# First pair's q and k ahead of V, a VectorE mask for two pairs, and earlier casts in a windowed-attention and tanh-MLP kernel

## The chip, the cores and the metric

The kernel runs on one core of one Trainium2 chip. The metric is the device time of one execution in microseconds. Before the change it is 363.07 us, the median of three runs (362.23 to 364.77). The execution that was profiled took 361.24 us, and its trace spans 359.5 us from the first to the last instruction, at a mean granted TensorE clock of 0.967 of full speed.

Engines are named as in the profile: PE is the matrix engine (PEld its weight loads), DVE is VectorE, ACT is ScalarE, POOL is GpSimd, SP is SyncE. SP and ACT start DMAs through hardware descriptor generation (HWDGE), POOL through software descriptor generation (SWDGE).

## What is computed

Eight sequences (batches) of 576 positions, eight heads of 64. Attention is causal with a window of 64: a query sees itself and the 63 keys before it. The heads' outputs are put side by side (4608 tokens of 512), multiplied by w_in, passed through h - tanh(h), and multiplied by w_out. All inputs and the output are float32.

```python
def _attn_ref(q, k, v):                       # [8, 8, 576, 64] each
    scores = np.matmul(q, k.transpose(0, 1, 3, 2)) / np.sqrt(64)
    rel = pos[:, None] - pos[None, :]
    scores = np.where((rel >= 0) & (rel < 64), scores, -1e9)
    attn = softmax(scores)
    return np.matmul(attn, v)

def _moe_ref(x, w_in, w_out):                 # x: [4608, 512]
    h = x @ w_in                              # [4608, 2048]
    return (h - np.tanh(h)) @ w_out
```

## The kernel before

**Attention.** Work goes by head pair: pair g is batch g // 4, heads p and p + 4 of it, so there are 32 pairs. q and k of a pair are loaded with 96 rows of 6 positions (`load`, line 86), transposed on PE, and copied out of PSUM to `kT` and `qs` or `qT`. Queries are cut into nine blocks j of 64; block j needs the 128 keys that end with it. Scores come out transposed (keys on the partitions), ACT takes the exponential into `PT`, and a second matmul multiplies by v with a column of ones added, so the sum of the weights arrives with the product and DVE divides by it (`reciprocal` and `tensor_tensor`). Results go to `xs`, are transposed (`x_tr`) and land in `xT` for the MLP.

**Two forms.** The first two batches use head-by-head transposes of the loaded tile (`tr_heads`, line 240), and `tile_scores` (267), which hides the forbidden keys before the exponential: two extra matmuls of the tile `hide` with the identity add -2^30 to them in PSUM (line 271). Values come from `tile_pv` (283). From batch 2 on q and k are first cast to a layout with both heads side by side (`cast`, 107), transposed (`tr`, 250), scored without hiding (`scores`, 298), and multiplied by a 0/1 mask on DVE afterwards (`masking`, 306). That mask is a 128x64 bf16 tile which lives in PSUM bank 5 and is written once by a PE transpose of `seen` (`see`, 208). The last batch's transposes are made by DMA.

**v.** It is loaded with 72 rows of 8 positions, cast to `vb` (`cast_v`, 160), and copied by small DMAs inside SBUF into windows `vw`: `keys_v` (164) fills the lower half of each block's 128 keys, and `shift_v` on DVE (169) copies block j to the upper half of block j + 1; later batches get both halves by `windows_v` (153). For batch 0 v is loaded as float32 on the SP and ACT queues (`load_v_wide`, 145), while q and k come over POOL's queue and are cast to bf16 by the DMA.

**The MLP.** Tokens go in nine chunks of 512. For each of 16 slices of 128 hidden features, four matmuls with w_in make `h` (line 361), ACT takes tanh (366), DVE subtracts (`gT`, 373). Output rows are made by four times 16 matmuls with w_out (385), copied by ACT and stored.

**What sets the order.** The schedule is by hand (`tc.manual_schedule()`): every engine runs its instructions in the order in which the program issues them, and waits only for data and buffers. The program has two parts. A prologue (422 to 476) does the attention of batch 0: loads, 13 matmuls on zeros that keep PE busy (`warm`, 235), casts, transposes, scores, values. Then a loop runs over numbered slots (607): `OPS` says which group of four MLP matmuls stands in a slot (slots 0 to 31 hold w_in of chunk 0, 32 to 47 w_out of chunk 0, 48 to 63 w_in of chunk 1, 64 to 79 w_out of chunk 1, from 80 on w_in of chunk 2 and then w_in and w_out alternating), and `at(h, ...)` puts a piece of attention behind it. `std` (530) places a pair of batch 2 or 3: casts at `ck` and `cq`, transposes at `t` and `tk`, scores at `ss`, masking at `ms`, values at `p`. Casts of q and k for pairs 8 and 9 are on DVE, later ones on POOL. `pace` (411) makes POOL wait for a given slice of `gT` before it issues a batch's loads. There is one buffer for v (`vall`), one `vb`, three each for the cast tiles, and one PSUM bank (3) for most transposes.

Of the kernel before, what the change touches and what calls it, by code (L numbers as in the profile page):

```python
# [7 lines left out]
F32 = mybir.dt.float32  # L8
BF16 = mybir.dt.bfloat16
ALU = mybir.AluOpType  # L10
# [5 lines left out]
def kernel(  # L16
# [9 lines left out]
    nc = tc.nc  # L26
# [14 lines left out]
    ctx.enter_context(tc.manual_schedule())  # L41

    const = ctx.enter_context(tc.tile_pool(name="const", bufs=1))
    all_pool = ctx.enter_context(tc.tile_pool(name="all", bufs=2))
    v_pool = ctx.enter_context(tc.tile_pool(name="v", bufs=1))
    row_pool = ctx.enter_context(tc.tile_pool(name="row", bufs=3))
# [9 lines left out]

    ident = const.tile([128, 128], BF16, name="ident")
    tick = const.tile([1, 1], BF16, name="tick")
    seen = const.tile([64, 128], BF16, name="seen")
    mask = ps[:, 5, 480:512].bitcast(BF16)  # L60
    hide = const.tile([128, 2, 64], BF16, name="hide")
    WIDE = 1024, 1024
    w_in_sb = [const.tile([128, 4, n], BF16, name=f"wi{i}") for i, n in enumerate(WIDE)]
# [16 lines left out]
    def move(eng, o, i):  # L80
        if eng is nc.scalar:
            nc.scalar.activation(o, i, ACT.Copy)  # L82
        else:
            eng.tensor_copy(o, i)  # L84

    def load(g, n, eng):

        b, pr = divmod(g, NP)
        if (b, n) not in whole:
            whole[b, n] = all_pool.tile([P, H, E * D], BF16, tag=n, name=n + "all")  # L90
        t = whole[b, n][:, pr::NP]
        eng.dma_start(out=t, in_=(q if n == "q" else k)[b, pr::NP].rearrange("h (p e) d -> p h (e d)", e=E))  # L92
        stage[g, n] = t

# [47 lines left out]
        for pr in range(NP):  # L142
            stage[b, pr, "v"] = t[:, pr::NP]

    def load_v_wide(pr, eng):
        if (0, "v") not in whole:
            whole[0, "v"] = g_pool.tile([128, M, TOK], BF16, tag="gT", name="v32").rearrange("p m t -> p (m t)").bitcast(F32)[
                0:PV].rearrange("p (h c) -> p h c", h=H)
        t = whole[0, "v"][:, pr::NP]
        eng.dma_start(out=t, in_=v[0, pr::NP].rearrange("h (p e) d -> p h (e d)", e=EV))  # L150
        stage[0, pr, "v"] = t

    def windows_v(b, j, eng):
        if j == 0:
            keys_v(b, 0, eng)
        else:
            eng.dma_start(out=vw[b % 2][:, j].rearrange("p h c -> p (h c)"),
                          in_=vb[8 * j - 8:8 * j + 8].rearrange("p e h c -> p e (h c)"))

    def cast_v(b, pr, eng=nc.gpsimd):  # L160
        move(eng, vb[:, :, 2 * pr:2 * pr + 2, 0:D].rearrange("p e h d -> p h e d"),
             stage.pop((b, pr, "v")).rearrange("p h (e d) -> p h e d", d=D))
# [43 lines left out]
                                base=64, pattern=[[-1, 128]], channel_multiplier=1)  # L206

    def see():
        nc.tensor.transpose(mask, seen, ident[0:64, 0:64])

    nc.vector.memset(qT[0], 0.0)
    nc.vector.memset(ident, 0.0)
# [22 lines left out]
    def warm(n):  # L235

        for _ in range(n):
            nc.tensor.matmul(ps[:, 7, :], qT[0][:, 0, 0:128], qT[0][:, 0, 0:512], start=True, stop=True)
# [25 lines left out]
        a, b = banks  # L264
        return ps[:, a:b + 1:b - a]

    def tile_scores(g, grp, banks):

        j0, n = (0, 5) if grp == 0 else (5, 4)
        for h in range(2):  # L270
            nc.tensor.matmul(ps[:, banks[h], 0:64 * n], ident, hide[:, h].unsqueeze(1).to_broadcast([128, n, 64]),  # L271
                             start=True, stop=False)
        for i in range(n):
            j = j0 + i
            for h in range(2):
                r = slice(64 * h, 64 * h + 64)
                nc.tensor.matmul(ps[:, banks[h], 64 * i:64 * i + 64], kT[g % NR][r, 64 * j:64 * j + 128],  # L277
                                 qs[g % 2][r, 64 * j:64 * j + 64], start=False, stop=i == n - 1)
        o = PT[g % NPT][:, j0:j0 + n].rearrange("p j (h t) -> p h j t", h=2)
        nc.scalar.activation(o, pair_of(banks)[:, :, 0:64 * n].rearrange("p h (j t) -> p h j t", t=64),  # L280
                             ACT.Exp, scale=scale)

    def tile_pv(g, banks):

# [67 lines left out]
    gT = {}  # L352
# [55 lines left out]
    def at(h, fn, *args):  # L408
        items.setdefault(h, []).append((fn, args))
# [9 lines left out]

    V, A, G, Y = nc.vector, nc.scalar, nc.gpsimd, nc.sync  # L420

    for pr in range(NP):
        load_v_wide(pr, (Y, A)[pr % 2])
    load(0, "k", G)
    load(0, "q", G)
    make_ident()
    load(1, "k", G)
    load(1, "q", G)
# [2 lines left out]
    load(2, "k", G)  # L431
    load(2, "q", G)

    warm(13)
    for pr in range(NP - 1):
        cast_v(0, pr, V)
    cast_v(0, 3, A)
    for j, eng in enumerate((Y, G, A, G, Y, A, G, Y, G)):
        keys_v(0, j, eng)
    for n in "kq":  # L440
        load(3, n, G)
# [7 lines left out]
        load(g, "q", G)  # L449
    load(7, "k", G)  # L450

    tr_heads(0, "k", 2, V)
    tr_heads(0, "q", 3, A)
    tile_scores(0, 0, (0, 1))
    tile_scores(0, 1, (4, 5))
    tr_heads(1, "k", 2, V)
    tr_heads(1, "q", 3, A)
    tr_heads(2, "k", 2, V)
    tile_scores(1, 0, (0, 1))
    tile_scores(1, 1, (4, 5))  # L460
    tr_heads(2, "q", 3, V)
    shift_dve(0, 0, 4)
    tile_pv(0, (6, 7))
    tr_heads(3, "k", 2, V)
    tile_scores(2, 0, (0, 1))
    tile_scores(2, 1, (4, 5))
    tr_heads(3, "q", 3, A)
    tile_pv(1, (6, 7))
    tile_scores(3, 0, (0, 1))
    tile_scores(3, 1, (4, 5))  # L470
    x_tr(0, 0, 0, 4, 0, A)
    x_tr(0, 0, 4, 9, 1, A)
    tile_pv(2, (2, 3))
    tile_pv(3, (6, 7))
    x_tr(0, 1, 0, 4, 4, V)
    x_tr(0, 1, 4, 9, 5, A)

    at(32, more_constants)
    at(33, lambda: [cast_v(1, pr, V) for pr in range(NP)])
    at(34, see)  # L480
    at(35, lambda: [keys_v(1, j, G) for j in range(NJ)])
    at(35, load, 7, "q", G)
    at(35, load_v_all, 2)
# [31 lines left out]
    for g in 10, 11:  # L515
        at(49, load, g, "k", G)
        at(49, load, g, "q", G)
    at(60, load_v_all, 3)
    for g in range(12, 16):
        at(g + 49, load, g, "k", G)  # L520
        at(g + 49, load, g, "q", G)
    for i in range(2):
        at(76 + 2 * i, more_zeros, i)

    def whole_pv(g):
        for i in range(3):
# [1 line left out]
        norm(g)  # L528

    def std(g, ck, cq, t, tk, ss, ms, p):  # L530
        at(ck, cast, g, "k", V if g < 10 else G)
        at(cq, cast, g, "q", V if g < 10 else G)
        at(t, tr, g, "q", 3, A, V)
        at(tk, tr, g, "k", 3, A)
        for i in range(3):
            at(ss + 2 * i, scores, g, i, 4)
        at(ms, masking, g)
        at(p, whole_pv, g)

    for i, g in enumerate(range(8, 12)):  # L540
        a = (50, 55, 60, 65)[i]
        std(g, a - 1, a - 2 if i < 2 else a - 2, a, a + 2, a + 3, a + 8, a + (12 if i == 0 else 11))
    at(70, x_tr, 2, 0, 0, 4, 3, V)
    at(71, x_tr, 2, 0, 4, 9, 3, A)
    at(78, x_tr, 2, 1, 0, 4, 3, V)
# [2 lines left out]
    for g in range(3 * NP, B * NP):  # L548
        b, pr = divmod(g, NP)
        a = 8 * g - 48 - (0, 2, 4)[min(b - 3, 2)]  # L550
        s = 32 * b - (0, 2, 4)[min(b - 3, 2)]
        cv, ky = s - 72 + 5 * pr, s - 54
        if b == 3:
            a = (65, 71, 76, 81)[pr]
            cv = 63 + pr
        elif b == 4:
            a = 82 + 7 * pr
            cv, ky = 74 + 3 * pr, 85
        elif b == 5:
# [97 lines left out]
```

The softmax here doesn't subtract the row's maximum and nothing guards it: scores larger than these inputs give would overflow.

## Time and profile before

| engine | busy us | share of the span |
|---|---|---|
| PE | 322.7 | 90% |
| DVE | 196.3 | 55% |
| ACT | 184.8 | 51% |
| POOL | 113.5 | 32% |

PE's busy time is mostly the MLP's: 145.1 us for w_in (576 matmuls) and 139.6 us for w_out. A busy time is the union of the intervals in which instructions of a kind run, so it counts a matmul at half clock twice as long. The page cuts the span into 40 slices of 9 us; the digits are tenths of the slice:

```profile
PE   5777999789776979699999999998999999999995
...
POOL 6730154757851742280172325801000000000000
PEclk9559999999999889999999999999999999999999
DMA  7999969696879146905769599488830410010021
```

Slices 1 and 2 (9 to 27 us) are at a clock of 0.5, two slices in the middle at 0.8. The DMA engines are busy for nine tenths from 9 us on until 45 us.

The groups of the operations that the change moves, adds or drops:

| operation | count in the stretch | mean ns |
|---|---|---|
| DVE cast of v to `vb`, 72x1024 from float32 | 3 | 700 |
| ACT cast of v to `vb`, 72x1024 from float32 | 1 | 1088 |
| PE `hide` matmul, 128x320 and 128x256, first 46 us | 8 and 8 | 444 and 375 |
| DVE mask multiply, 128x1152, whole run | 24 | 746 |
| POOL cast of q or k, 96x768 | 40 | 829 and 834 |
| DVE cast of q or k, 96x768 | 4 | 346 |

### The profile page before, as it was taken

The numbers are of one execution on the slowest core, as the hardware profiler recorded it, in microseconds if no ns is written. First come the engines' busy times: TensorE is split into PE (matmuls) and PEld (weight loads), VectorE is DVE, ScalarE is ACT, GpSimd is POOL, SyncE is SP. The second block draws the span as 40 slices with busy tenths as digits, with TensorE's granted clock in tenths as the row PEclk, the third lists the DMA queues.
The fourth block names the chain that finished last, engine by engine and source line by source line (L and its number), as shares of the span: only waits on it lengthen the run. The fifth ranks groups of instructions, "written<-read, shape, count | busy, mean of one in ns | idle before, by whom it ended". The sixth has DMA issues, their size and how long they took to land.

```text
span 359.5 us, 6211 instructions
## 1 busy us (share of the span) xinstructions
PE 322.7 (90%) x2407; PEld 178.0 (50%) x2438; DVE 196.3 (55%) x317; ACT 184.8 (51%) x334; POOL 113.5 (32%) x168
## 2 busy tenths in 40 slices
PE   5777999789776979699999999998999999999995
PEld 1454545546443445465555555554555444444442
DVE  3255743667834477867677666655666334433300
ACT  1445715478543558556666666654554443444411
POOL 6730154757851742280172325801000000000000
PEclk9559999999999889999999999999999999999999
DMA  7999969696879146905769599488830410010021
GB/s 175 155 199 216 195 107 155 103 180 99 128 115 255 44 81 102 170 3 113 137 120 184 112 151 191 100 145 191 203 109 30 96 60 29 29 60 29 29 79 70
DMA packets 51310, 42.69 MB, mean 119 GB/s; under 512 B 20848, under 2 KB 44080, under 8 KB 51280
## 3 DMA queue, kind: packets, MB, share of 16 engines
q0 software_dynamic: 21072, 19.77, 35.9%
q1 hardware_dynamic: 29752, 21.79, 24.9%
q10 hardware_dynamic: 456, 0.72, 0.7%
q8 instruction: 19, 0.31, 0.3%
q14 instruction: 11, 0.09, 0.1%
HBM read 36.70 MB, written 11.21 MB: 133 GB/s over the span
## 4 chain that ended last, share of the span: by engine, by line
PE 74%; DVE 8%; DMA 7%; ACT 5%; issue 2%; POOL 2%; ACTq 1%; SPq 0%; DVEq 0%; POOLq 0%
PE ps L385 33%; PE ps L361 28%; DMA qall<-in_q_dram 4%; PE ps L314 3%; PE ps L302 3%; DMA v<-in_v_dram 2%; PE ps L254 2%; DVE xs L325 2%; DVE gT L373 2%; PE ps L246 2%; PE ps L271 1%; ACT th L366 1%; PE ps L277 1%; DVE xs L296 1%; PE ps L331 1%
## 5 line engine op out<-in xcount | busy, mean ns | idle before, releaser
L361 PE MATMUL ps<-xT,wi 128*128 128x512 bf16 x576 | 145.1, 381 | 3.8 <-DVE gT L373 3.1
L373 DVE TENSOR_TENSOR gT<-ps,th 128x512 bf16<-128x512 f32 x144 | 98.4, 691 | 85.6 <-ACT th L366 83.8
L385 PE MATMUL ps<-w_out_sb,gT 128*128 128x512 bf16 x545 | 139.6, 382 | 2.4 <-issue 0.8
L366 ACT ACTIVATE th<-ps 128x512 f32<-128x512 f32 x144 | 85.7, 598 | 75.1 <-PE ps L361 73.3
L361 PEld LDWEIGHTS <-wi 128*128 128x128 bf16 x576 | 61.7, 113 | 51.1 <-issue 5.6
L385 PEld LDWEIGHTS <-gT 128*128 128x128 bf16 x576 | 53.7, 98 | 56.2 <-issue 2.0
L304 ACT ACTIVATE pt<-ps 128x384 bf16<-128x384 f32 x72 | 35.3, 490 | 38.0 <-PE ps L302 37.8
L84 POOL COPY vb<-vall 72x1024 bf16<-72x1024 bf16 x24 | 25.0, 1055 | 42.5 <-DMA vall<-in_v_dram 30.9
L325 DVE TENSOR_TENSOR xs<-ps,rc 64x576 bf16<-64x576 f32 x48 | 36.2, 755 | 1.1
L390 ACT ACTIVATE ysb<-ps 128x512 f32<-128x512 f32 x36 | 21.6, 599 | 21.9 <-PE ps L385 21.7
L302 PE MATMUL ps<-qt,kt 128*128 128x128 bf16 x216 | 24.0, 220 | 3.5 <-ACT pt L304 1.6
L314 PEld LDWEIGHTS <-pt 128*128 128x128 bf16 x216 | 16.7, 98 | 15.3 <-issue 2.0
L314 PE MATMUL ps<-vw,pt 128*128 128x130 bf16 x216 | 21.4, 220 | 2.3 <-DVE xs L325 1.9
L302 PEld LDWEIGHTS <-kt 128*128 128x128 bf16 x216 | 16.5, 98 | 13.0 <-issue 3.6
L84 DVE COPY qt<-ps 64x576 bf16<-64x576 bf16 x20 | 15.2, 760 | 13.5 <-ACT qt L82 13.4
L84 POOL COPY qb<-qall 96x768 bf16<-96x768 bf16 x18 | 14.9, 829 | 14.6 <-DMA qall<-in_q_dram 14.6
L308 DVE TENSOR_TENSOR pt<-pt,ps 128x1152 bf16<-128x1152 bf16 x24 | 17.9, 746 | 1.4 <-ACT pt L304 1.4
L84 POOL COPY kb<-kall 96x768 bf16<-96x768 bf16 x22 | 18.2, 834 | 0.0
L280 ACT ACTIVATE pt<-ps 128x640 bf16<-128x640 f32 (+1 forms) x16 | 10.3, 650 | 13.9 <-PE ps L277 13.9
L84 DVE COPY kt<-ps 128x576 bf16<-128x576 bf16 x8 | 6.0, 756 | 18.4 <-PE ps L246 18.4
L92 POOL DMA_DIRECT2D kall<-in_k_dram x16 | 11.2, 702 | 11.0 <-DMA wi<-in_moe_w_in_dram 5.4
L82 ACT ACTIVATE kt<-ps 128x576 bf16<-128x576 bf16 x20 | 13.0, 648 | 2.0 <-PE ps L254 1.9
(64 smaller groups left out, 195.8 us busy)
## 6 DMA issues: line engine op xcount, KB each, us to landing
out_dram<-ysb SPq DMA_DIRECT2D x36, 256.0 KB
vw<-vb SPq DMA_DIRECT2D x40, 130.0 KB
vall<-in_v_dram POOLq DMA_DIRECT2D x7, 576.0 KB, 10.0
kall<-in_k_dram POOLq DMA_DIRECT2D x16, 144.0 KB, 7.4
qall<-in_q_dram POOLq DMA_DIRECT2D x16, 144.0 KB, 7.4
kall<-in_k_dram POOLq DMA_DIRECT2D x4, 576.0 KB, 6.3
qall<-in_q_dram POOLq DMA_DIRECT2D x4, 576.0 KB, 8.6
wi<-in_moe_w_in_dram POOLq DMA_DIRECT2D x2, 1024.0 KB, 13.5
```

Source lines behind the costliest of these rows:

```text
L82: nc.scalar.activation(o, i, ACT.Copy)
L84: eng.tensor_copy(o, i)
L302: nc.tensor.matmul(sp[:, i, :], kT[g % NR][:, 64 * j:64 * j + 128], qT[g % NR][:, :, 64 * j:64 * j + 64], start=True, stop=True)
L304: nc.scalar.activation(PT[g % NPT][:, 3 * grp:3 * grp + 3, :], sp, ACT.Exp, scale=scale)
L308: nc.vector.tensor_tensor(p, p, mask.unsqueeze(1).to_broadcast([128, 2 * NJ, 64]), ALU.mult)
L314: nc.tensor.matmul(ps[:, 5 + grp, 130 * i:130 * i + 130], PT[g % NPT][:, j, :], vw[b % 2][:, j, 2 * pr:2 * pr + 2, :], start=True, stop=True)
L325: nc.vector.tensor_tensor(xo[r, :, :, pr, :], ov[r, :, :, h, 0:D], rc[r].to_broadcast([64, 3, 3, 64]), ALU.mult)
L361: nc.tensor.matmul(hp, w_in_tile(ki, m), chunk_tile(c)[:, :, ki % 2, 64 * (ki // 2):64 * (ki // 2) + 64], start=(ki == 0), stop=(ki == 3))
L366: nc.scalar.activation(th, hp, ACT.Tanh)
L373: nc.vector.tensor_tensor(gT[c][:, m, :], hp, th, ALU.subtract)
L385: nc.tensor.matmul(yp, gT[c][:, m, s * 128:(s + 1) * 128], w_out_sb[:, m, :], start=(m == 0), stop=(m == M - 1))
L390: nc.scalar.activation(ysb, ps[:, yp_bank(c, s), :], ACT.Copy)
```

## The change

It has four parts.

1. **Start.** The first pair's q and k are loaded first, as float32, q on SP's and k on ACT's queue, and cast by DVE and ACT (`cast_flat`). The four loads of v move to POOL's queue, which casts to bf16 (`load_v`), ahead of the other pairs. `warm` shrinks from 13 to 9 matmuls. The casts of v to `vb` all go to DVE, behind the first pair's k copy and ahead of the others. The small DMAs of v's keys are issued after the first pair's scores, five on POOL, three on SP and one on ACT (before: four, three and two).
2. **Mask.** `tile_scores` has three forms. Pair 0 hides as before. Pairs 1 and 2 ("mask") leave out the hiding matmuls, and DVE multiplies `PT` by the mask after the exponential. For pair 3 ("hidden") the hiding matmuls stand ahead of the scores as a step of their own. So `see` runs in the prologue, with a 128x128 `seen`, and the mask moves within bank 5. Pair 0's values come after pair 2's scores, pairs 1 to 3 follow together, and two `warm` matmuls stand between the two halves of the final transposes.
3. **Casts.** In batches 2 and 3 the casts come three to six slots ahead of the transposes (before: one and two), q ahead of k. Those of pairs 12, 13 and 14 go from POOL to DVE; 10, 11 and 15 stay on POOL.
4. **Slots.** Loads of v and of pairs 12 to 15 are issued earlier, the transposes of batch 3 start at slots 68, 73, 78 and 82 (before 65, 71, 76 and 81), batch 4's two slots later, and the memsets of `qz` move from slots 76 and 78 to 140 and 144.

The diff, cut to what these parts need:

```diff
+    qk_pool = ctx.enter_context(tc.tile_pool(name="qk", bufs=1))
...
-    seen = const.tile([64, 128], BF16, name="seen")
-    mask = ps[:, 5, 480:512].bitcast(BF16)
+    seen = const.tile([128, 128], BF16, name="seen")
+    mask = ps[:, 5, 448:480].bitcast(BF16)
...
-        if (b, n) not in whole:
-            whole[b, n] = all_pool.tile([P, H, E * D], BF16, tag=n, name=n + "all")
-        t = whole[b, n][:, pr::NP]
+        if g == 0:
+            t = qk_pool.tile([P, 2, E * D], F32, tag=n, name=n + "f")
+        else:
+            if (b, n) not in whole:
+                whole[b, n] = all_pool.tile([P, H, E * D], BF16, tag=n, name=n + "all")
+            t = whole[b, n][:, pr::NP]
...
-    def load_v_wide(pr, eng):
-        if (0, "v") not in whole:
-            whole[0, "v"] = g_pool.tile([128, M, TOK], BF16, tag="gT", name="v32").rearrange("p m t -> p (m t)").bitcast(F32)[
-                0:PV].rearrange("p (h c) -> p h c", h=H)
-        t = whole[0, "v"][:, pr::NP]
-        eng.dma_start(out=t, in_=v[0, pr::NP].rearrange("h (p e) d -> p h (e d)", e=EV))
-        stage[0, pr, "v"] = t
+    def load_v(b, pr):
+        if (b, "v") not in whole:
+            whole[b, "v"] = v_pool.tile([PV, H, EV * D], BF16, tag="v", name="vall")
+        t = whole[b, "v"][:, pr::NP]
+        nc.gpsimd.dma_start(out=t, in_=v[b, pr::NP].rearrange("h (p e) d -> p h (e d)", e=EV))
+        stage[b, pr, "v"] = t
...
+    def cast_flat(g, n, eng):
+        t = row_pool.tile([P, E, 2, D], BF16, tag=n + "b", name=n + "b").rearrange("p e h d -> p (e h d)")
+        t = t.rearrange("p (h c) -> p h c", h=2)
+        move(eng, t, stage.pop((g, n)))
+        stage[g, n] = t
...
-    def tile_scores(g, grp, banks):
+    def tile_scores(g, grp, banks, how="hide"):
...
+        if how == "hide":
+            hides(grp, banks)
...
+        if how == "mask":
+            p = PT[g % NPT][:, j0:j0 + n].rearrange("p j (h t) -> p (j h) t", h=2)
+            nc.vector.tensor_tensor(p, p, mask.unsqueeze(1).to_broadcast([128, 2 * n, 64]), ALU.mult)
...
+    load(0, "q", Y)
+    load(0, "k", A)
     for pr in range(NP):
-        load_v_wide(pr, (Y, A)[pr % 2])
-    load(0, "k", G)
-    load(0, "q", G)
+        load_v(0, pr)
     make_ident()
...
-    warm(13)
-    for pr in range(NP - 1):
+    warm(9)
+    cast_flat(0, "q", V)
+    cast_flat(0, "k", A)
+    tr_heads(0, "k", 2, V)
+    tr_heads(0, "q", 3, A)
+    see()
+    for pr in range(NP):
         cast_v(0, pr, V)
-    cast_v(0, 3, A)
-    for j, eng in enumerate((Y, G, A, G, Y, A, G, Y, G)):
+    tile_scores(0, 0, (0, 1))
+    tile_scores(0, 1, (4, 5))
+    for j, eng in enumerate((Y, G, A, G, Y, G, G, Y, G)):
         keys_v(0, j, eng)
...
-    tile_scores(1, 0, (0, 1))
-    tile_scores(1, 1, (4, 5))
-    tr_heads(2, "q", 3, V)
+    tile_scores(1, 0, (0, 1), "mask")
+    tile_scores(1, 1, (4, 5), "mask")
+    tr_heads(2, "q", 3, A)
+    tile_scores(2, 0, (0, 1), "mask")
+    tile_scores(2, 1, (4, 5), "mask")
+    tr_heads(3, "k", 2, V)
     shift_dve(0, 0, 4)
     tile_pv(0, (6, 7))
-    tr_heads(3, "k", 2, V)
-    tile_scores(2, 0, (0, 1))
-    tile_scores(2, 1, (4, 5))
     tr_heads(3, "q", 3, A)
+    hides(0, (0, 1))
+    hides(1, (4, 5))
+    tile_scores(3, 0, (0, 1), "hidden")
+    tile_scores(3, 1, (4, 5), "hidden")
     tile_pv(1, (6, 7))
...
+    warm(2)
...
-    at(60, load_v_all, 3)
+    at(49, load_v_all, 3)
     for g in range(12, 16):
-        at(g + 49, load, g, "k", G)
-        at(g + 49, load, g, "q", G)
+        at(60 + (g - 12) // 2, load, g, "k", G)
+        at(60 + (g - 12) // 2, load, g, "q", G)
     for i in range(2):
-        at(76 + 2 * i, more_zeros, i)
+        at(140 + 4 * i, more_zeros, i)
...
-        at(ck, cast, g, "k", V if g < 10 else G)
-        at(cq, cast, g, "q", V if g < 10 else G)
+        at(cq, cast, g, "q", V if g not in (10, 11, 15) else G)
+        at(ck, cast, g, "k", V if g not in (10, 11, 15) else G)
...
         if b == 3:
-            a = (65, 71, 76, 81)[pr]
-            cv = 63 + pr
+            a = (68, 73, 78, 82)[pr]
+            cv = 62 + pr
         elif b == 4:
-            a = 82 + 7 * pr
-            cv, ky = 74 + 3 * pr, 85
+            a = 84 + 7 * pr
+            cv, ky = 75 + 3 * pr, 86
...
-            std(g, a - 1, a - 2, a, a + 2, a + 3, a + 8, a + 11)
+            lead = 3 if pr < 3 else 6
+            std(g, a - lead + 1, a - lead, a, a + 2, a + 3, a + 8, a + 11)
```

More of the change, by code (lines that the diff above doesn't have):

```diff
@@ L208, in see @@
     def see():
-        nc.tensor.transpose(mask, seen, ident[0:64, 0:64])
+        nc.tensor.transpose(ps[:, 5, 448:512].bitcast(BF16), seen, ident)
     nc.vector.memset(qT[0], 0.0)
@@ L265, in pair_of, with hides @@
         return ps[:, a:b + 1:b - a]
-    def tile_scores(g, grp, banks):
-        j0, n = (0, 5) if grp == 0 else (5, 4)
+    GROUPS = (0, 5), (5, 4)
+    def hides(grp, banks):
+        n = GROUPS[grp][1]
         for h in range(2):
@@ L272, in tile_scores @@
                              start=True, stop=False)
+    def tile_scores(g, grp, banks, how="hide"):
+        j0, n = GROUPS[grp]
+        if how == "hide":
+            hides(grp, banks)
         for i in range(n):
@@ L277, in tile_scores @@
                 nc.tensor.matmul(ps[:, banks[h], 64 * i:64 * i + 64], kT[g % NR][r, 64 * j:64 * j + 128],
-                                 qs[g % 2][r, 64 * j:64 * j + 64], start=False, stop=i == n - 1)
+                                 qs[g % 2][r, 64 * j:64 * j + 64], start=how == "mask", stop=how == "mask" or i == n - 1)
         o = PT[g % NPT][:, j0:j0 + n].rearrange("p j (h t) -> p h j t", h=2)
@@ L450 @@
     load(7, "k", G)
[L452 to L455, printed above, removed]
     tr_heads(1, "k", 2, V)
@@ L458 @@
     tr_heads(2, "k", 2, V)
-    tile_scores(1, 0, (0, 1))
-    tile_scores(1, 1, (4, 5))
-    tr_heads(2, "q", 3, V)
+    tile_scores(1, 0, (0, 1), "mask")
[4 more added lines that the diff above has]
+    tr_heads(3, "k", 2, V)
     shift_dve(0, 0, 4)
     tile_pv(0, (6, 7))
-    tr_heads(3, "k", 2, V)
-    tile_scores(2, 0, (0, 1))
-    tile_scores(2, 1, (4, 5))
     tr_heads(3, "q", 3, A)
+    hides(0, (0, 1))
+    hides(1, (4, 5))
+    tile_scores(3, 0, (0, 1), "hidden")
+    tile_scores(3, 1, (4, 5), "hidden")
     tile_pv(1, (6, 7))
[L469 to L472, printed above, removed]
     tile_pv(2, (2, 3))
[L474 to L478, printed above, removed]
+    tile_pv(3, (0, 1))
+    x_tr(0, 0, 0, 4, 4, A)
+    x_tr(0, 0, 4, 9, 5, A)
+    warm(2)
+    x_tr(0, 1, 0, 4, 6, V)
+    x_tr(0, 1, 4, 9, 3, A)
     at(33, lambda: [cast_v(1, pr, V) for pr in range(NP)])
-    at(34, see)
+    at(34, more_constants)
     at(35, lambda: [keys_v(1, j, G) for j in range(NJ)])
@@ L541 @@
         a = (50, 55, 60, 65)[i]
-        std(g, a - 1, a - 2 if i < 2 else a - 2, a, a + 2, a + 3, a + 8, a + (12 if i == 0 else 11))
+        lead = 3 if i < 2 else 5
+        std(g, a - lead + 1, a - lead, a, a + 2, a + 3, a + 8, a + (12 if i == 0 else 11))
     at(70, x_tr, 2, 0, 0, 4, 3, V)
```

## Prediction

> **What bounds the kernel now.** I first read busy time by stage, since the page's mean (PE busy for 90% of the span) hides where the other tenth goes. Columns: stretch, its length, busy us and count of PE, PEld, DVE, ACT, POOL, then granted clock, DMA share, GB/s.
>
> ```profile
> 0.00:31.00 31.00, 20.33 (x298) 12.19 (x299) 13.02 (x27) 11.04 (x17) 16.02 (x30) 0.72 0.97 182
> 31.00:53.00 22.00, 21.40 (x110) 10.50 (x109) 13.54 (x23) 10.95 (x20) 5.71 (x10) 1.00 0.95 165
> 53.00:70.00 17.00, 15.69 (x288) 9.47 (x290) 7.27 (x13) 8.59 (x15) 10.01 (x15) 1.00 0.81 137
> 70.00:92.00 22.00, 19.32 (x142) 11.48 (x144) 15.90 (x29) 16.40 (x33) 14.65 (x23) 1.00 0.85 139
> 92.00:150.00 58.00, 45.00 (x366) 26.96 (x368) 34.74 (x57) 30.60 (x61) 28.42 (x39) 0.94 0.72 124
> 185.00:320.00 135.00, 133.11 (x805) 71.80 (x819) 78.93 (x121) 73.26 (x130) 25.69 (x39) 1.00 0.54 113
> ```
>
> From 185 us on PE is full (133.11 of 135), so what happens there is PE work, which the change leaves alone. PE idles 10.7 us in the first 31 (at a clock of 0.72), and 13.0 us from 92 to 150. The change touches exactly these two stretches. Next the timeline of the first, start and length in us:
>
> ```profile
> 9.66 0.69 PE L246 MATMUL ps<-ident,kall 96*64 96x96 bf16 x12 [3.53 <-DMA kall<-in_k_dram]
> 11.99 0.65 ACT L82 ACTIVATE qs<-ps 128x576 bf16<-128x576 bf16 x1 [1.46 <-DVE kt L84]
> 13.18 0.70 ACT L280 ACTIVATE pt<-ps 128x640 bf16<-128x640 f32 x1 [0.54 <-PE ps L277]
> 19.59 1.33 DVE L172 COPY vw<-vw 64x2080 bf16<-64x2080 bf16 x2
> 30.41 2.75 PE L361 MATMUL ps<-xT,wi 128*128 128x512 bf16 x12
> ```
>
> The first transposes wait for k until 9.66; the chain of waits runs through v's last load (7.94 us), its cast and two issues on ACT. The first exponential starts at 13.18, and the first w_in matmul at 30.41. In the answer on w_in's tile its halves land 10.8 and 16.1 us after their issue at 14.43 and 15.2, so at 25.2 and 31.3: w_in does not hold the start, attention does.
>
> For the second stretch I read the chain of waits (start, length, what):
>
> ```profile
> 75.01 7.11 DMA qall<-in_q_dram
> 82.94 0.83 POOL kb L84
> 83.77 0.78 POOL vall L141
> 85.18 6.97 DMA qall<-in_q_dram
> 92.29 0.83 POOL qb L84
> 94.31 0.85 POOL kb L84
> 95.17 0.41 PE ps L254 x6
> ```
>
> and PE's waits between 88 and 150 (total us, times, longest):
>
> ```profile
> PE ps L314 <- DVE xs L325: 1.9, 1, 1.9
> PE ps L331 <- DVE qt L84: 1.8, 1, 1.8
> PE ps L254 <- POOL kb L84: 1.7, 1, 1.7
> PE ps L254 <- ACT xT L82: 1.7, 2, 0.9
> PE ps L302 <- ACT pt L304: 1.6, 3, 0.6
> ```
>
> The first view shows one POOL queue: load, cast, load, cast, each behind a 7 us landing. The second shows that only 2.0 us are charged to POOL directly (1.7, and 0.3 for qb); the rest is turnaround on ACT and DVE where transposes and scores are packed too tightly between few w_out matmuls.
>
> **What the Trainium skill says.** "DMA: Bandwidth & Descriptors", section "SWDGE vs HWDGE vs iDMA": a cast inside a DMA is possible only from GpSimd. So q and k over SP and ACT must land as float32 and be cast by an engine; v as bf16 by GpSimd is allowed. The trace agrees as far as it goes: v over SP and ACT lands as f32 here. "TensorE: Matmul & The Clock Gate", "What's actually happening": PE gets its full clock after a window of about 3.4 us of activity and loses it after an idle one. Here the warm matmuls take 427 ns at first and 213 ns from 4.9 us, and after the 3.53 us gap twelve transposes take 0.69 against 0.45 us at full clock. "VectorE: DVE Perf Modes", "Why PSUM operands drop a tier": 16-bit operands in PSUM still allow two elements a cycle. The mask multiply agrees: 1152 elements in 0.746 us.
>
> **The start, worked out.** q0 and k0 take the place of v's first two loads on SP and ACT. Those landed at or before 5.70 and 6.36 (two DVE casts back to back from 5.70); size is the same (2 x 576 x 64 floats), and GpSimd's third stream runs beside them as before. So q0 and k0 land at about 5.7 to 6.3. Casts: 72x1024 f32 took 1.09 on ACT and 0.70 on DVE; for 768 elements 0.85 and 0.55. k's transposes can start at 6.6 to 7.2, say 7.0, against 9.66.
>
> From there: kt's copy starts 0.75 after the transposes (10.40 against 9.66) and takes 0.76; qs no longer waits for the v cast and two issues on ACT, so it ends near 9.0; the first exponential runs at about 9.6 against 13.18, a lead of 3.6. hide (here made at 5.1) comes after four v issues and two more: about 6.9, hidden. seen is one more transpose of 0.2 us.
>
> Then the loads set the pace. v's four loads stand first in GpSimd's queue; vall(1), as much data, took 3.8 us alone (landed 44.9, w_out at 41.1). With the sharing until 6, v is there at about 8.8; k1, q1, k2, q2 at about 1 us each land from 9.8 to 12.8. ACT is the next chain, estimated from the rows above (0.65 a copy, 0.70 and 0.60 an exponential): pair 1's exponentials end at 14.7, pair 2's at 17.2. Before it was 18.7 and 24.5, because each pair also waited for hide matmuls (0.71 and 0.61 at half clock, gone for two pairs) and pair 2 stood behind pair 0's values. The price is four mask multiplies on DVE: 1152 elements cost 0.746, so 640 and 512 cost between the proportional 0.41 and 0.33 and the full 0.75; I take 0.48 and 0.41, 1.8 us in all. They stand ahead of kt(3), the shift and all four normalisations in DVE's order, so they are on the path.
>
> DVE then: masks to 17.6, kt(3) to 18.4, shift (1.33) to 19.7. PE's values of pair 0 follow, then pair 3's q transposes, copy, scores and exponentials to about 23.6 (3.9 us, as before), then four normalisations of 1.05, of which three come behind pair 3's scores: 23.3 + 3.15 = 26.45. Transposes and copy 0.6: the first w_in matmul at 27.0. With full clock throughout it would be 25.4. w_in is issued at about 13.8 and lands near 24 to 25, so it doesn't bind. warm(9) ends near 5.2, which leaves a gap of 1.8 us, so I count on half clock, and on perhaps 0.5 us lost before the w_in matmuls are at full clock. Gain of the start: 30.4 to 26.9, **3.5 us**; bounds 0 (a late v) and 5.2.
>
> Does it survive until 53? DMA keeps its old schedule: w_out's second half lands at 41.1 and vall(1) at 44.9. The w_out matmuls would start at 41.4, their third part later, so they just fit. vb's casts shift from 47.5 only to 45, and POOL's chain by 2.5 us. In the 70 to 92 stretch cast(10) was done at 83.8 while PE wanted it at 87.0, a slack of 3.2, so PE keeps the 3.5 there.
>
> **The middle.** Casts of pairs 12, 13 and 14 go from POOL to DVE: six of 0.83 off POOL (5.0 us), six of 0.35 on DVE (2.1 us), beside DVE's 23 idle us in 92 to 150. Moving two memsets of 1.38 to slots 140 and 144 frees POOL of another 2.8 there. vall(3) is asked for before the casts of pair 10. DVE's new casts at slot 65 and later wait for q12 and k12, behind which masks and normalisations queue; these loads are issued at about 81 and land by 87, PE is at slot 65 at 89, so they are there. v(3)'s casts end near 92 instead of 98.9, its windows and vall(4) come 7 us earlier, and POOL's 11.6 us wait for vall(4) (to 115.5) ends near 108, ahead of PE's need at slot 82. So POOL drops off the path: 2.0 us. The later slots (65, 71, 76, 81 become 68, 73, 78, 82; the fourth batch's two later) spread the turnarounds; of the other 11 us idle I take a fifth, 2 us. The two half-clock stretches (117.6 to 120.6 and 131 to 134, about 2.3 us lost) follow gaps of 1.87 and 1.80; I take 0.5. Sum **4.5 us**; bounds 1 (only new places for the same turnarounds) and 8.
>
> Nothing comes after: 185 to 320 is full. 363.1 - 3.5 - 4.5 = **355.0**.
>
> **Rivals.** (1) Only the start pays; the middle waits on ACT and DVE copies wherever the slots are, since the wait list names them for most of the idle time: 363.1 - 3.5 - 0.5 = 359. (2) Only the middle pays: v behind q and k arrives at 12 instead of 9, DVE stands on its cast with kt(1) behind, keys and w_in are issued 3 us later, and PE begins near 30: 363.1 - 4 = 359. Against it: v's 3.8 us alone. (3) Both pay in full, full clock at the start: 363.1 - 5.2 - 7 = 351. (4) Slower: late v, and the DVE casts on pairs 12 to 14 block gT and normalisations on landings of 7 us, twice: 363.1 + 1 + 4 = 368. For it: a DMA share of 0.88, 0.96 and 0.99 in 70 to 80, 100 to 110 and 110 to 120; against it: those loads are issued earlier than before.
>
> **How the numbers follow.** Main case (353 to 357.5) 0.5, full gain 0.14, one of two halves 0.24, slower 0.07, nothing net 0.05. The halves lie about the 1% line at 359.4, some under it: faster by over 1% 0.80, within 1% 0.14, slower 0.06. The range takes in the full gain and the halves: 350.5 to 360.5.
>
> **What would show it.** First k transposes near 7, first exponential before 10, the shift before 20.5, first w_in matmul at 26 to 27.5; no POOL releaser in PE's waits from 88 on; PE idle in that 58 us stretch down from 13 to about 9; the tail of the last 170 us unchanged in length. I am wrong if the w_in matmuls wait for DMA, if DVE's idle before its q and k casts is over 1 us a time, or if half-clock stretches grow.

## The result, and the profile after

The changed kernel takes 351.49 us (median of four runs, 349.35 to 353.63) against 363.92 us for the kernel before on the same chip (362.23 to 365.05). The ratio is 0.966, with an interval of 0.959 to 0.974. The profiled executions span 359.5 us before and 347.6 us after; the latter is the fastest of its four. Ratios, here and below, leave out runs that lie over 1.5% above the fastest of their kernel, which among others is the profiled run of `start_only` (364.17 us).

I first split the 11.9 us between the stages by the start of the same w_in matmul in both traces:

| w_in matmul (slot) | before, us | after, us | lead, us |
|---|---|---|---|
| first of chunk 0 (0) | 30.41 | 28.02 | 2.4 |
| first of chunk 1 (48) | 71.75 | 69.12 | 2.6 |
| last of chunk 1 (63) | 90.76 | 88.04 | 2.7 |
| first of chunk 2 (80) | 123.27 | 111.96 | 11.3 |
| sixteen matmuls later | 132.43 | 116.94 | 15.5 |
| first of chunk 3 | 152.41 | 139.95 | 12.5 |
| the last | 340.43 | 328.77 | 11.7 |
| end of the span | 359.50 | 347.64 | 11.9 |

So 2.4 us come from the start, 8.6 us from one place, slots 64 to 79 (w_out of chunk 1), and almost nothing from the rest. The lead of 15.5 is no gain: in the slots just behind 80 the kernel before already does attention work of batch 4, with a wait of 1.80 us behind a copy to `qt`, which the kernel after does a few slots later; 2.5 us of the lead are given back within the next sixteen matmuls.

The windows of the kernel after, with the columns used in the prediction, for three of its stretches:

```profile
0.00:31.00 31.00, 21.21 (x298) 12.84 (x299) 14.45 (x33) 12.90 (x22) 17.67 (x33) 1.00 0.98 172
92.00:150.00 58.00, 49.08 (x418) 29.48 (x415) 41.25 (x70) 36.10 (x72) 22.99 (x33) 1.00 0.68 120
185.00:320.00 135.00, 134.12 (x786) 70.94 (x785) 75.16 (x116) 70.98 (x125) 22.55 (x32) 1.00 0.48 104
```

The clock column can't be taken at its word in the first stretch: it reads 1.00, but the twelve transposes at 6.28 (below) take 0.69 us, as those before the change did at half clock. PE's idle time from 92 to 150 fell from 13.0 to 8.9 us (58 less the busy time), and the full tail stayed full. But fixed windows mislead once work has moved by 11 us between them: this one now holds 418 PE records where it held 366. The stretch that counts is bounded by slots. Here are slots 64 to 79, from the end of chunk 1's last w_in group to the first of chunk 2, in the kernel before and then the kernel after:

```profile
91.14:123.27 32.13, 23.87 (x201) 14.09 (x203) 16.89 (x27) 13.44 (x26) 17.84 (x24) 0.95 0.80 144
88.42:111.96 23.54, 21.34 (x194) 12.70 (x191) 16.37 (x29) 12.15 (x26) 9.32 (x14) 1.00 0.95 176
```

The stretch is 8.6 us shorter. PE's idle time in it went from 8.26 to 2.20 us; the other 2.5 us is shorter busy time. An estimate: `slots_pool`, below, has the slots of before at a clock of 1.00 and is busy for 22.70 us, so about 1.2 of the 2.5 us is the clock of these two executions; the rest is perhaps work that went two slots on, which no run separates. POOL's busy time halves, 17.8 to 9.3 us, which looks like the reason and, as the experiments show, is not it.

PE's waits in the kernel after, from 88 to 112 us (total, times, longest):

```profile
PE ps L263 <- DVE xT L85: 1.3, 2, 0.8
PE ps L350 <- DVE qt L85: 0.7, 1, 0.7
PE ps L321 <- ACT pt L323: 0.2, 1, 0.2
```

No POOL releaser is left, and the waits of 1.9 us on `xs`, 1.7 on `kb`, and 1.6 on `pt` that led the list before are gone or small. Last, the start in the timeline of the kernel after (start, length, then idle time and releaser in brackets):

```profile
6.28 0.69 PE L255 MATMUL ps<-ident,kb 96*64 96x96 bf16 x12 [0.65 <-POOL hide L206]
8.68 0.70 ACT L296 ACTIVATE pt<-ps 128x640 bf16<-128x640 f32 x1 [0.54 <-PE ps L293]
...
14.10 0.37 PE L293 MATMUL ps<-qs,kt 64*128 64x64 bf16 x7 [1.29 <-DVE pt L300]
...
19.80 1.31 DVE L181 COPY vw<-vw 64x2080 bf16<-64x2080 bf16 x2
...
28.02 2.75 PE L380 MATMUL ps<-xT,wi 128*128 128x512 bf16 x12
```

The first transposes moved from 9.66 to 6.28, the first exponential from 13.18 to 8.68: 4.5 us ahead. The shift of v, which stood at 19.59, stands at 19.80. So the whole lead is spent by then; what is left of it at the w_in matmuls (2.4 us) comes from the shorter work after the shift, where only pair 3 has to be scored. The score matmul at 14.10 waits 1.29 us for DVE's mask multiply, which itself waits for an exponential; that was not foreseen.

### The profile page after: what moved, and what is told of

The parts are those of the page before. It is cut to its first block, busy times and chain, and to the rows that moved or that the text cites. A ratio compares the mean times of both kernels' runs of the same rounds, so it can differ in the third digit from the quotient of the medians.

```text
span 347.6 us, 6234 instructions
## 1 busy us (share of the span) xinstructions
PE 319.6 (92%) x2428; PEld 175.9 (51%) x2428; DVE 199.2 (57%) x328; ACT 184.8 (53%) x335; POOL 110.9 (32%) x165
## 4 chain that ended last, share of the span: by engine, by line
PE 79%; DVE 8%; ACT 5%; DMA 3%; issue 3%; POOL 1%; SPq 0%; DVEq 0%; POOLq 0%; ACTq 0%
PE ps L404 34%; PE ps L380 31%; PE ps L321 3%; PE ps L333 3%; PE ps L263 2%; DVE gT L392 2%; DMA kt<-kd 2%; DMA kall<-in_k_dram 2%; PE ps L255 2%; DVE xs L344 2%; DVE qt L85 1%; ACT th L385 1%; PE ps L293 1%; ACT pt L323 1%; DVE xs L315 1%
## 5 line engine op out<-in xcount | busy, mean ns | idle before, releaser
L404 PE MATMUL ps<-w_out_sb,gT 128*128 128x512 bf16 x576 | 143.5, 379 | 0.0
L85 POOL COPY qb<-qall 96x768 bf16<-96x768 bf16 x15 | 12.4, 830 | 10.8 <-DMA qall<-in_q_dram 10.8
L85 POOL COPY kb<-kall 96x768 bf16<-96x768 bf16 x19 | 15.8, 834 | 0.0
L96 POOL DMA_DIRECT2D qall<-in_q_dram x15 | 10.0, 668 | 12.2 <-DMA wi<-in_moe_w_in_dram 6.2
```

Source lines behind the costliest of these rows:

```text
L404: nc.tensor.matmul(yp, gT[c][:, m, s * 128:(s + 1) * 128], w_out_sb[:, m, :], start=(m == 0), stop=(m == M - 1))
```

## The experiments

All times are medians, the ratio is to the kernel before, run on the same chip, with its 95% interval. The theory that I held going in was that of the prediction. Its rival was that the middle is set by how densely the slots pack transposes and scores, wherever the casts are.

### The two halves apart

`start_only` is the prologue of the changed kernel with the old loop.

```diff
 # prologue (loads, casts, mask for pairs 1 and 2, hidden pair 3): as after
-    at(33, ...) and all further slots of after
+    at(32, ...) and all further slots of before, without at(34, see)
```

> The changed prologue (q and k first, v behind, mask for two pairs) with the loop of before. If the two halves add up, the first w_in matmul stands near 28.0 us as in the changed kernel and the lead of 2.4 us is still there at the end: 361.5 us, ratio 0.993. If the middle of before is bound by loads and casts on POOL that keep their own time, the lead is lost by slot 80 and the time is that of before, 363.9. A gain over 4 us would mean that the prologue also frees the middle.

Measured: 360.65 us (357.67 to 364.17) against 363.61, ratio 0.987 (0.980 to 0.994). The first w_in matmul starts at 28.40.

`middle_only` is the other half: the old prologue, the new loop.

```diff
 # prologue: as before
-    at(32, ...) and all further slots of before
+    at(33, ...) and all further slots of after, with at(34, see)
```

> The prologue of before with the changed loop (earlier casts, casts of pairs 12 to 14 on DVE, later slots, loads earlier, memsets later). If the halves add up: the first w_in matmul at 30.4 us, the stretch of slots 64 to 79 down from 32.5 to about 24 us, in all 354.5 us, ratio 0.974. If the earlier start is needed for the middle to run free (loads in time), under 5 us of gain: 359 or more.

Measured: 354.09 us, ratio 0.973 (0.968 to 0.978). The first w_in matmul starts at 30.75; slots 64 to 79 take 23.7 us, as in the full change.

The halves are worth 3.0 and 9.5 us, together 12.5, which is what the whole is worth (12.4). They add, with no sign that either needs the other, and about three quarters lie in the loop. The intervals are wide: 2 to 7 us for the start, 8 to 12 for the loop.

### Is it the casts on DVE?

`casts_pool` undoes only the move of the casts of pairs 12 to 14.

```diff
-        at(cq, cast, g, "q", V if g not in (10, 11, 15) else G)
+        at(cq, cast, g, "q", V if g < 10 else G)
-        at(ck, cast, g, "k", V if g not in (10, 11, 15) else G)
+        at(ck, cast, g, "k", V if g < 10 else G)
```

> The changed kernel, but casts of pairs 12, 13 and 14 stay on POOL, at the changed slots. If the engine of these six casts is what freed the stretch of slots 64 to 79, that stretch goes back from 23.9 towards 30 us and the time rises by 4 to 7 us, to 356 to 358. If the earlier cast slots and the later transposes do it, POOL has time enough and the time stays within 1.5 us of 351.5.

Measured: 349.69 us (348.69 to 350.24), ratio 0.960 (0.955 to 0.964). Giving all six casts back to POOL costs nothing. In its trace slots 64 to 79 end at 112.24 (111.96 with the casts on DVE), and PE waits for POOL nowhere between 88 and 113. So the DVE casts aren't the reason.

### Is it the slots?

`slots_back` keeps everything but the slots. `slots_pool` does the same with the casts on POOL, so that the two questions can be told apart.

```diff
-            a = (68, 73, 78, 82)[pr]
+            a = (65, 71, 76, 81)[pr]
...
-            a = 84 + 7 * pr
+            a = 82 + 7 * pr
```

> The changed kernel, but the transposes of batch 3 start at slots 65, 71, 76, 81 and batch 4's two slots earlier, as before, each with its casts the same lead ahead. If the crowding of transposes between few w_out matmuls was the cost, PE's waits in slots 64 to 79 come back and the time rises by 3 to 6 us, to 354.5 to 357.5. If the casts on DVE and the earlier loads do it, the time stays within 1.5 us of 351.5.

> As the run with the slots of before for batches 3 and 4, but casts of pairs 12 to 14 on POOL, so that no DVE cast can stand beside POOL's v casts (one took 2.20 us there). If crowding of two pairs in the same slots is the cost, the time stays at 360 to 364 and slots 64 to 79 take 31 us or more. If the slow DVE cast made that run slow, the time falls to 352 to 355.

Measured: `slots_back` 363.85 us, ratio 0.998 (0.996 to 1.001), slower than either expectation: with the old slots the whole change, its start included, brings nothing. `slots_pool` took 358.74 us (358.27 to 358.81), ratio 0.987 (0.982 to 0.991), between its two expectations and nine us above `casts_pool`, from which it differs only in the slots. Its window over slots 64 to 79 and PE's longest waits in it, 88 to 122 us:

```profile
89.60:120.65 31.05, 22.70 (x207) 13.59 (x205) 16.90 (x27) 13.43 (x26) 16.55 (x24) 1.00 0.84 148
```

```profile
PE ps L333 <- DVE xs L344: 1.9, 1, 1.9
PE ps L263 <- POOL qb L85: 1.7, 1, 1.7
PE ps L321 <- ACT pt L323: 1.6, 3, 0.6
PE ps L263 <- ACT kt L83: 0.9, 1, 0.9
```

PE idles 8.35 us (31.05 less 22.70), as before the change (8.26), and the list is that of before with other line numbers: 1.9 on `xs`, 1.7 on POOL, 1.6 on `pt`. Yet this kernel has the new start, the casts further ahead and the earlier loads. What those waits share is the slots.

`slots_back` is another 5 us slower and differs from `slots_pool` only in the DVE casts: they have a price that the new slots hide. Its timeline, POOL, DVE and PE (start, length):

```profile
88.97 4.15 POOL L85 COPY vb<-vall 72x1024 bf16<-72x1024 bf16 x4
...
90.01 2.20 DVE L85 COPY qb<-qall 96x768 bf16<-96x768 bf16 x1
...
95.31 0.64 PE L263 MATMUL ps<-ident,qb 96*128 96x96 bf16 x6 [4.21 <-DVE qt L85]
```

A DVE cast that takes 0.35 us elsewhere takes 2.20 beside POOL's casts of v, with masks and `gT` queued behind it; PE then stands 4.21 us. The Trainium skill, "SBUF — State Buffer", section "SBUF: two separate sides", says that DVE, in its two-port modes or with two SBUF inputs, and GpSimd share one pair of ports as an exclusive lock, and that the loser blocks for the other's whole instruction. The trace agrees with that (the cast starts beside POOL's casts of about 1.04 each and takes about as long as two of them); no run here isolates it, and how the 5 us divide is open. In the kernel after, the same cast comes at 92.44, as POOL's casts of v end, and takes 0.36.

### Which slot?

`pair12_back` is `casts_pool` with pair 12 alone at its old slot.

```diff
-            a = (68, 73, 78, 82)[pr]
+            a = (65, 73, 78, 82)[pr]
```

> The changed kernel with POOL casts and only pair 12's pieces back at slot 65, where pair 11's stand too; the other pairs keep the changed slots. If the collision of pairs 11 and 12 on one slot (two transposes of q through one bank, then two of k, then scores, then values) is the cost, most of it comes back: 356 to 361. If the spread of all four pairs and of batch 4 does it, under 3 us come back: 350 to 353.

Measured: 356.16 us (355.93 to 357.89), ratio 0.981 (0.976 to 0.985), 6.5 us above `casts_pool`. One pair, three slots earlier, is about 70% of the effect of the slots. PE idles 7.2 us in slots 64 to 79, and the waits of the list above come back: 1.9 on `xs`, 1.7 on `qt`, 1.7 on `pt`, 0.9 on `kt`. One of them in the timelines of the kernel before, of `pair12_back` and of `slots_pool`, in that order, each with the DVE copy that ends just ahead of it:

```profile
94.36 0.76 DVE L84 COPY qt<-ps 64x576 bf16<-64x576 bf16 x1
95.17 0.41 PE L254 MATMUL ps<-ident,qb 96*128 96x96 bf16 x6 [1.72 <-POOL kb L84]
```

```profile
91.81 0.76 DVE L85 COPY qt<-ps 64x576 bf16<-64x576 bf16 x1
92.63 0.41 PE L263 MATMUL ps<-ident,qb 96*128 96x96 bf16 x6 [1.72 <-DVE qt L85]
```

```profile
92.84 0.76 DVE L85 COPY qt<-ps 64x576 bf16<-64x576 bf16 x1
93.67 0.43 PE L263 MATMUL ps<-ident,qb 96*128 96x96 bf16 x6 [1.73 <-POOL qb L85]
```

One wait of 1.72 us has three names. At slot 65 the q transposes of pair 12 come right behind the q transposes of pair 11, both into PSUM bank 3, and both pairs go through the same slots up to their values at slot 76. What fills the 1.72 us every time is the bank being emptied: ACT and then DVE copy `qt` out of it, DVE behind a mask multiply and a `gT`, and DVE's copy ends at 95.12, 92.57 and 93.60, within 0.1 us of PE's start. POOL is named when it happened to end last. In the kernel before it is named with a cast of k that these q transposes don't read; the cast of q that they read had ended at 93.12. (In `slots_pool` that cast ends at 93.62, so there both were due at once.) This is the wait that the prediction booked as POOL's.

### The earlier loads

`loads_back` keeps the new slots and the DVE casts but issues the loads of v and of pairs 12 to 15, and the memsets, where they were before.

```diff
-    at(49, load_v_all, 3)
+    at(60, load_v_all, 3)
-        at(60 + (g - 12) // 2, load, g, "k", G)      # and "q"
+        at(g + 49, load, g, "k", G)                  # and "q"
-        at(140 + 4 * i, more_zeros, i)
+        at(76 + 2 * i, more_zeros, i)
```

> The changed kernel with v(3), the loads of pairs 12 to 15 and the two memsets at the slots of before. If loads in time matter beside the slots, DVE's casts of pairs 12 to 14 wait for landings and the time rises by 2 us or more, to 353.5 or above. If POOL had slack, it stays within 1.5 us of 351.5.

Measured: 352.68 us (350.90 to 355.56), ratio 0.971 (0.965 to 0.978). That overlaps the full change (0.959 to 0.974): a loss of up to some 3 us can't be ruled out, one of 9 can. Slots 64 to 79 are 1.4 us longer in its trace.

`slots_only` asks the opposite: the kernel before with nothing changed but the slots.

```diff
-            a = (65, 71, 76, 81)[pr]
+            a = (68, 73, 78, 82)[pr]
...
-            a = 82 + 7 * pr
+            a = 84 + 7 * pr
```

> The kernel before with one part of the change alone: batch 3's transposes at slots 68, 73, 78, 82 and batch 4's two slots later; prologue, casts (one and two slots ahead, on POOL), loads and memsets as before. If the slots carry the middle, slots 64 to 79 take 24 to 26 us instead of 32.5 and the time is 354 to 357. If loads and cast leads are needed too, POOL becomes the releaser in PE's waits and the time is 358 to 361.

Measured: 360.90 us against 362.90, ratio 0.996 (0.993 to 0.999). The slots that are worth 9 us in the changed kernel are worth 2 here. Its timeline says why:

```profile
115.89 1.04 POOL L84 COPY vb<-vall 72x1024 bf16<-72x1024 bf16 x1 [11.41 <-DMA out_dram<-ysb]
...
118.19 0.82 POOL L84 COPY qb<-qall 96x768 bf16<-96x768 bf16 x1
119.07 0.66 PE L254 MATMUL ps<-ident,qb 96*128 96x96 bf16 x6 [6.59 <-POOL qb L84]
```

PE runs ahead into pair 15, whose cast stands in POOL's queue behind a cast of v that waits 11.41 us for `vall(4)`. PE stands 6.59 us, and this time it is POOL's wait in truth: the q cast ends at 119.01, PE starts at 119.07.

So two limits lay over each other in these slots: dense slots, and POOL's queue. Freeing POOL alone (`slots_pool` against `start_only`) brings 358.74 against 360.65, a difference that isn't shown, since both ratios are 0.987; moving the slots alone brings about 2; both bring 9.5 (`middle_only`). For POOL's queue, either the casts on DVE (`loads_back`) or the earlier issues (`casts_pool`) do nearly all, and both aren't needed. Both runs keep the casts further ahead of the transposes; no run takes that part away alone.

### The start: bank 5, pair 3's keys, and v's queue

PE's two waits of 1.29 us (14.10 and 17.65) fall where the second group of scores of pairs 1 and 2 goes into bank 5, in which the mask also lies that DVE is reading. The Trainium skill, "PSUM — Partial Sum Buffer", section "PSUM bank collisions raise a hardware error ⚠️", says that two engines may not be in one bank and the same 32 partitions at a time, even at different addresses, so such accesses must be ordered. The trace shows what the ordering costs here: PE waits for the exponential of the first group (0.70 us) and the multiply behind it (0.49). `banks46` moves that group to bank 6.

```diff
-    tile_scores(1, 1, (4, 5), "mask")
+    tile_scores(1, 1, (4, 6), "mask")
-    tile_scores(2, 1, (4, 5), "mask")
+    tile_scores(2, 1, (4, 6), "mask")
```

> The changed kernel, but the second score group of pairs 1 and 2 goes to banks 4 and 6 instead of 4 and 5. In the changed kernel PE stood twice 1.29 us before the matmuls that write bank 5, released by DVE's mask multiply, which reads the mask in bank 5. If that bank sharing makes the wait, both gaps vanish and the first w_in matmul comes 1 to 2.2 us sooner (26 to 27 us), 349.5 to 350.5 in all. If the values or DVE's chain hold the end of the prologue, the gaps vanish and the first w_in matmul moves by less than 0.5 us.

Measured: 350.35 us (349.21 to 352.23, six runs), ratio 0.964 (0.960 to 0.968), the same as the full change. Its timeline:

```profile
12.82 0.66 PE L293 MATMUL ps<-qs,kt 64*128 64x64 bf16 x18
...
14.63 0.60 ACT L296 ACTIVATE pt<-ps 128x512 bf16<-128x512 f32 x1 [0.62 <-DVE pt L300]
...
18.52 0.69 PE L255 MATMUL ps<-ident,kall 96*64 96x96 bf16 x12 [2.04 <-DMA kall<-in_k_dram]
```

The eighteen score matmuls of pair 1 now run without a break, so the cause of PE's 1.29 us is shown. The edit doesn't remove the whole wait: the second group's exponential still stands 0.62 us behind the first group's multiply, and why is not shown. Nothing is gained at the end of the prologue, because PE then waits 2.04 us for the keys of pair 3, whose load is behind five small DMAs in POOL's queue. The first w_in matmul starts at 28.41.

`k3_early` puts the loads of pair 3 ahead of those small DMAs and leaves the banks alone.

```diff
     load(2, "q", G)
+    load(3, "k", G)
+    load(3, "q", G)
...
-    for n in "kq":
-        load(3, n, G)
```

> The changed kernel with pair 3's k and q loads issued ahead of the keys of v instead of behind them on POOL's queue. If pair 3's k, which lands near 18 us, holds back kt(3) and with it the shift and the values, the shift moves from 19.8 to 18.5 or sooner and the first w_in matmul by up to 1.3 us. If the exponentials and masks of pairs 1 and 2, which end at 19.0, hold it, it moves by under 0.4 us.

Measured: 351.86 us, ratio 0.971 (0.965 to 0.976). The shift starts at 19.64 and the first w_in matmul at 28.02: no gain either.

`v_hw` brings v as float32 over SP and ACT behind the first q and k, instead of through POOL.

```diff
-        load_v(0, pr)
+        load_v_wide(pr, (Y, A)[pr % 2])
```

> The changed kernel, but v comes as float32 over SP and ACT behind q and k, and POOL's queue starts with pair 1's k and q. If v over POOL's queue ahead of the other pairs is what lets the start go, v's casts end later, the keys and shift with them, and the first w_in matmul stands at 28.5 to 30 us: 352 to 353.5. If only q and k first matters, k1 lands before 9 instead of 10.05, and the first w_in matmul stays within 0.5 us of 28.0, or is sooner.

Measured: 351.87 us (351.56 to 355.96), ratio 0.975 (0.968 to 0.982), an interval that overlaps that of the full change, so the times don't separate them. The traces do:

```profile
11.89 0.69 PE L263 MATMUL ps<-ident,kall 96*64 96x96 bf16 x12 [3.26 <-DMA kall<-in_k_dram]
```

Pair 1's keys, now first in POOL's queue, still land only at 11.89 (10.05 in the kernel after, where four loads of v stand ahead of them), and the first w_in matmul starts at 30.77 (28.02 in the kernel after). These 2.8 us are still missing at slot 80 (114.73 against 111.96). The move of v to the other two queues is the only edit, so it delays these keys; how it does so is not shown.

### Both obstacles of the start removed

`best` is `casts_pool` with the edits of `banks46` and `k3_early`.

> Pair 3's loads early, the second score group of pairs 1 and 2 in banks 4 and 6, and POOL casts for pairs 12 to 14. Taking the bank wait away alone moved nothing, since PE then stood on pair 3's k (2.04 us at 18.52). If these two waits cover each other, taking both away moves the shift to about 18 and the first w_in matmul to 26 to 27: 348 to 349.5. If ACT's order of copies and exponentials is the bound, the first w_in matmul stays at 27.5 or later: 349.5 to 351.

Measured: 348.85 us (347.21 to 350.10, six runs), ratio 0.963 (0.959 to 0.967). The shift in its timeline:

```profile
18.77 1.38 DVE L181 COPY vw<-vw 64x2080 bf16<-64x2080 bf16 x2
```

With both edits the shift starts a microsecond sooner (19.80 in the kernel after) and the first w_in matmul at 27.05, against 28.02. Kernels whose prologue is that of the change start it between 28.02 and 28.89, so this is outside the spread. The two obstacles covered each other. But of the 0.97 us only 0.55 is left at the first matmul of chunk 1 (68.57 against 69.12), and nothing sixteen matmuls later (73.87 against 73.92). Between these two lies a stretch at low clock, in this execution:

```profile
68.57:72.30 3.73, 3.73 (x15) 1.55 (x14) 0.82 (x4) 1.92 (x5) 2.31 (x5) 0.69 0.95 158
69.12:72.35 3.23, 2.75 (x16) 1.34 (x13) 0.91 (x4) 1.92 (x5) 3.05 (x6) 1.00 0.90 118
```

The first line is `best`, the second the kernel after. The time of `best` can't be told from that of `casts_pool` or of the full change; no other run here is faster.

## Why the prediction was right, and where it was not

The forecast was 355.0 with a range of 350.5 to 360.5; the time is 351.49. So the gain was 12.4 us where 8.0 was forecast: the start brought less than forecast, the middle twice as much and more than its upper bound of 8, and the two errors cancel in part. It lies at the number of rival 3 (351), but not by its road: that gave the start 5.2 us and the middle 7, and they brought 2.4 and about 9. That the two agree is luck.

**The start, up to pair 1: right.** q0 and k0 were to be cast from 5.7 to 6.3, and their casts started at 5.18 and 5.38 (0.56 and 0.84 long, as taken). Transposes were put at 7.0 and came at 6.28; the first exponential at 9.6 and came at 8.68; k1 at 9.8 and came at 10.05. Pair 1's exponentials were to end at 14.7 and ended at 15.10. The multiplies cost 0.49 and 0.42 (0.48 and 0.41 taken).

**The start, from pair 2 on: 1.1 us too much.** The step that failed is "ACT is the next chain", with pair 2's exponentials ending at 17.2; they ended at 18.66. The masks were priced as DVE time in DVE's order, but not as a reader of bank 5, in which they, and the exponentials that they wait for, hold up PE's scores by 1.29 us a time. The shift came at 19.80 instead of 18.4 (kt(3) before it), and the first w_in matmul at 28.02 instead of 27.0. The prediction didn't look at pair 3's loads behind the small DMAs either; `banks46`, `k3_early` and `best` show that both had to go for the microsecond to come back. The sum also took pair 3's exponentials at 23.6 and then went on from 23.3. The first half of w_in landed at about 25.9 and did not bind.

**Survival until 53: right.** The 2.4 us are 2.6 at slot 48. Whether there is room for more is not shown: of `best`'s further 0.97 us, 0.55 is left there.

**"So POOL drops off the path: 2.0 us": the outcome was right, the reason wrong.** POOL's times were right (casts of v(3) to end near 92, and ended at 92.6; the wait for `vall(4)` to end near 108, and ended at 109.8), and no POOL releaser is left. The step that failed is taking the releaser's name for the cause: 1.72 of the 2.0 us was the turnaround of bank 3, which the slots removed. It is there with POOL relieved (`slots_pool`) and in `pair12_back` goes under DVE's name. And the six casts moved to DVE weren't needed for it (`casts_pool`).

**"Of the other 11 us idle I take a fifth, 2 us": the term that was mis-sized.** The slots are worth 9 us once POOL's queue is out of the way: `slots_pool` to `casts_pool`, 358.74 to 349.69. The prediction saw that the waits were turnaround "where transposes and scores are packed too tightly", and had no step that counted which pairs stand in the same slots. Pair 12 at 65 beside pair 11 is 6.5 us of it by itself. The half clock (0.5 us taken) is gone in this execution (0.94 to 1.00 from 92 to 150), but not for want of gaps: `slots_pool` keeps them, the one of 1.9 us included, at a clock of 1.00 in slots 64 to 79.

**The added wait on DVE: right for these slots only.** The casts of pairs 12 to 14 didn't stand on landings. With the old slots one of them takes 2.20 us beside POOL's casts, and the whole gain is lost (`slots_back`): DVE held up by these casts, as in the slower rival, but not by landings.

**The test "PE idle in that 58 us stretch down from 13 to about 9"** came out at 8.9, and proves little: part of the gain lies before 92, and the window holds other work than before.

What stays open: how much of the loss in `slots_back` is the port and how much the order of DVE's queue; the size of the loads' own part, between 0 and 3 us; and what the earlier casts are worth by themselves.

## What to carry to other kernels

When many short waits in one stage name different engines, look for the buffer or bank that the waiting instructions share, and for the two pieces of work that a schedule puts into the same slots: moving one of them by three slots was worth more here than taking five microseconds of work off an engine. Undo the parts of a change one at a time and also do each alone, because two limits at the same place hide each other in both directions (about 2 and nothing clear alone, 9.5 together; at the end of the prologue nothing and nothing alone, one together). Compare stages by the same instruction in both traces, not by the same microseconds.

## What the hardware showed that was not expected

- A DVE copy of 96x768 bf16 from SBUF to SBUF took 2.20 us beside POOL's copies of 1.04, and 0.35 to 0.37 in the kernel after.
- A DVE multiply of 0.49 us that reads its 0/1 factor from a PSUM bank held up matmuls into other columns of that bank by 1.29 us, since they also waited out the exponential ahead of it (0.70).
- PE's clock at the first transposes differs between kernels with the same prologue: twelve took 0.69 us in the kernel after and 0.45 in `casts_pool`. The faster ones brought nothing: the first w_in matmuls start at 28.02 and 28.59.
- A wait of 1.9 us was followed by matmuls at half clock in the kernel before (117.6 to 120.6, as the prediction has it) and not in `slots_pool`.
- A load of 0.3 MB that stood first in GpSimd's queue landed at 11.89 us beside float32 loads on SP and ACT, later than behind four loads of v in its own queue (10.05).
